# A two-layer attention and feed-forward kernel: other PSUM banks for the second projection, places of their own for its last copies, an earlier normalization, a maximum in two parts, and another order in the score rounds

## The chip, the cores and the metric

The kernel runs on one core of one Trainium2 chip. The metric is the device time of one execution in microseconds. Before the change it is 1984.87 us, the median of 3 runs that lie between 1984.5 and 1985.03 us.

## The reference

The input is one sequence of 2048 rows of 448 numbers. Attention has 16 query heads of width 28 that share one key and one value head of width 28. Two layers are run, each an attention block and then a gated feed-forward block, and both layers use the same weights:

```python
def _A_ref(x, wq, wk, wv, wo):
    q = (x @ wq).reshape(B, S, H, Dh).transpose(0, 2, 1, 3)
    k = x @ wk
    v = x @ wv
    scores = jnp.einsum("bhqd,bkd->bhqk", q, k) * (Dh ** -0.5)
    p = _softmax(scores, axis=-1)
    o = jnp.einsum("bhqk,bkd->bhqd", p, v)
    return o.transpose(0, 2, 1, 3).reshape(B, S, H * Dh) @ wo

def _B_ref(x, w_gate, w_up, w_down):
    return (_silu(x @ w_gate) * (x @ w_up)) @ w_down

x = A_x
for _ in range(2):
    x = x + _A_ref(_layernorm(x), A_wq, A_wk, A_wv, A_wo)
    x = x + _B_ref(_layernorm(x), B_w_gate, B_w_up, B_w_down)
```

`_layernorm` subtracts the mean of a row and divides by the root of its variance plus 1e-5. There is no scale and no bias.

## The kernel before

**Number formats.** A product in near-float32 precision is made of a high and a low part of each operand (`hi`, `lo`, type F32R) and three matmuls: high by high, high by low, low by high.

**Chunks.** The 2048 rows are four chunks (`c` = 0 to 3) of 512 rows, and a chunk is four tiles of 128 rows. PSUM has eight banks of 128 x 512 numbers. The order of the instructions on each engine is the order in which the program writes them (`manual_schedule`): there is no scheduler between, and an instruction that waits holds up all that stands behind it on its engine.

**The projection of a layer** (`project`, L493) has 16 steps, counted by `seen` from 0 to 15. Steps 4c to 4c+3 make one chunk's queries, keys and values: each is 11 matmuls of 128 x 512 into one bank (L312), which ScalarE then copies out twice, first the high part (L530), then the whole bank into a tile called `stage` (L531); SyncE's queue sends `stage` to DRAM (`qd`, and `kt` for the keys). Two of each chunk's four steps also have VectorE turn the value rows out of the bank (`vt`, L538), and GpSimd puts them into `vsb`. The order of the four steps in a chunk is `TURN` = (3, 2, 0, 1), and `LAST` = (1, 0, 2, 3) for chunk 3; the steps with a number below 2 are those that have a `vt`. `stage` has 3 buffers in layer 0 and 2 in layer 1.

The bank of a step comes from `bank(wide[-1], True)`, which takes the next free one of a list in turn; in the steps of `finish` the list is `ALL` = (4, 5, 6, 7, 0, 1, 2, 3). The last three steps take banks 3, 4 and 5:

```python
held, po = bank((3, 4, 5) if self.seen > len(self.order) - 4 else wide[-1], True)   # L516
```

**What stands between the steps.** `plan[n, 0]` is done ahead of step n and `plan[n, 1]` behind it. A chunk is normalized in parts (`norm_steps`, L211): `stat` for each of four tiles on VectorE (L217, L218), `scale` on GpSimd (L222 and, with a power of -0.5, L223), and `apply` for each of four tiles on VectorE (L230) with a small copy on GpSimd (L232). In layer 0 the statistics and the scale of chunk c stand behind step 4c-4 and the application behind step 4c-3. `flip` (L243) then turns the chunk by 16 transposes on TensorE (L248), ahead of the last step of the chunk before; ScalarE and VectorE split what they make into `xh` and `xl`. In layer 1 chunks 0 to 2 are turned on VectorE and sent through DRAM (`xt`); `parts` (L882, ahead of step 6 for chunk 2) splits what came back in `qstack`. Chunk 3 of layer 1 is applied ahead of step 8 (L857), and flipped ahead of step 11.

Steps 0 to 3 of layer 1 stand inside the last feed-forward groups of layer 0; steps 4 to 15 stand in `finish`, behind the last down-projection, whose sums lie in banks 4 to 7 until VectorE (L823) and ScalarE (L826) have taken them out.

`maxima` (L434) gives a bound on the scores of a chunk: 4 matmuls (L439), then on VectorE a transpose (L441), a reduction (L443), three small instructions (L447, L448, L450) and a DMA. For chunks 0 to 2 it stands behind steps 6, 10 and 14; for chunk 3 it stands between the first two cycles of the scores (L756).

**The scores** of a layer are 128 cycles, m = 0 to 127: 16 groups of queries by 8 cycles. A cycle (`cycle`, L613) handles two tiles of 128 keys. For each, `tile_scores` (L590) issues 3 rounds of 4 matmuls, one for each of four heads, in four row groups of the array (L597): heads 0 to 2 write the three banks of `three`, and head 3 writes a bank of its own, here called the single:

```python
for z, (kp, part) in enumerate(((0, 0), (1, 0), (0, 1))):
    for j in range(4):
```

ScalarE takes the exponential of each `three` (L619). VectorE copies each single into `pair` (L618), and ScalarE takes the exponential of both at once (L620). Behind the two tiles TensorE multiplies the probabilities of the cycle before by the values (`pv`, 16 matmuls, L652), and VectorE adds that up (L661, or a copy L659 in the first cycle of a group). There are two banks for all this, 6 and 7, and they change places in each cycle (`singles`, L609):

```python
return banks[6 + m % 2], banks[7 - m % 2]
```

The first tile's single and then, when VectorE has copied it, the product with the values go into the first of them; the second tile's single goes into the other, out of which VectorE first has to add up the product of the cycle before. Behind six of the cycles of the two layers TensorE also does an output projection (L582).

The feed-forward block after it is matmuls in two row groups (L332); the change does not touch it.

Of the kernel before, what the change touches and what calls it, by code (L numbers as in the profile page):

```python
# [8 lines left out]
F32 = mybir.dt.float32  # L9
# [6 lines left out]
P = 128  # L16
# [39 lines left out]
def forward(  # L56
# [81 lines left out]
    xres = pers.tile([P, NT, D], F32, name="xres")  # L138
    stats = pers.tile([P, NT, 6], F32, name="stats")
    mv = pers.tile([P, NT, 2], F32, name="mv")  # L140
    halfn = pers.tile([P, 4], F32, name="halfn")
    ident = pers.tile([P, P], F32, name="ident")
    vsb = pers.tile([P, NT, 32], F32, name="vsb")
    keys = [pers.tile([P, 2, 512], F32R, name=f"keys{c}") for c in range(NC)]
# [63 lines left out]
            again,  # L208
        )

    def norm_steps(c, pool=pers, twice=True):  # L211

        got = {}
        cs = slice(4 * c, 4 * c + 4)

        def stat(t):
            nc.vector.bn_stats(stats[:, 4 * c + t, :], xres[:, 4 * c + t, :])  # L217
            nc.vector.bn_aggr(mv[:, 4 * c + t, :], stats[:, 4 * c + t, :])  # L218

        def scale():  # L220
            rstd = pers.tile([P, 4], F32, name="rstd", bufs=2)
            nc.gpsimd.tensor_scalar(rstd, mv[:, cs, 1], 1.0, EPS, ALU.mult, ALU.add)  # L222
            nc.gpsimd.tensor_tensor(rstd, rstd, halfn, ALU.pow)  # L223
            got["r"] = rstd

        def apply(t):
            if t == 0:
                got["x"] = pool.tile([P, 4, 512], F32, name="xn")
            o, i, r = got["x"][:, t, 0:D], xres[:, 4 * c + t, :], got["r"][:, t : t + 1]
            nc.vector.tensor_scalar(o, i, mv[:, 4 * c + t, 0:1], r, ALU.subtract, ALU.mult)  # L230
            if twice:
                nc.gpsimd.tensor_copy(got["x"][:, t, D:512], o[:, 384:D])  # L232

        fs = [lambda t=t: stat(t) for t in range(4)] + [scale]
        return fs + [lambda t=t: apply(t) for t in range(4)], got

    def norm(c, pool=pers):
# [105 lines left out]
    class Attention:  # L343


        def __init__(self, layer):
            self.layer = layer
            self.squares = (0, 1, 2) if layer else ()
            self.X, self.norms, self.qd = {}, {}, {}
            self.done = 0  # L350
            self.order = [(c, m) for c in range(NC) for m in (TURN if c < NC - 1 else LAST)]
            self.seen = 0
            self.steps, self.places = [], []
            self.lent, self.plan = None, {}
            self.hi, self.rowsof, self.kt, self.when = {}, {}, {}, {}
            for c in range(NC):
                self.kt[c] = dram.tile([32, 512], F32, name=f"kt{layer}_{c}")
                self.at(4 * c + 4, lambda c=c: self.key_load(c))
                self.at(4 * c + 7, lambda c=c: self.key_split(c))
            for i in range(3):  # L360
                self.at(4 + 3 * i, lambda i=i: self.stack(i))
                self.at(6 + 3 * i, lambda i=i: self.parts(i))
# [70 lines left out]

        def maxima(self, c, pm=None):  # L434


            pm = bank(ALL)[1] if pm is None else pm
            for n, g in enumerate(TURN):
                nc.tensor.matmul(pm, kd[0:112, g, :], self.hi[c, g], start=(n == 0), stop=(n == 3))  # L439
            side = pers.tile([P, 512], F32, name="sg")  # L440
            nc.vector.transpose(side, pm)  # L441
            ng = pers.tile([P, 64], F32, name="ng")
            nc.vector.tensor_reduce(ng, side.rearrange("p (n k) -> p n k", k=8), AX.X, ALU.max, negate=True)  # L443
            two = pers.tile([P, 4, 2, 16], F32R, name="two")
            hi, lo = two[:, :, 0, :], two[:, :, 1, :]
            ng = ng.rearrange("p (b j) -> p j b", j=4)
            nc.vector.tensor_copy(hi, ng)  # L447
            nc.vector.tensor_tensor(lo, ng, hi, ALU.subtract)  # L448
            flat = pers.tile([P, P], F32, name="flat")
            nc.vector.transpose(flat, two.rearrange("p j z b -> p (j z b)").bitcast(F32))  # L450
            self.rowsof[c] = dram.tile([P, P], F32, name=f"rows{self.layer}_{c}")
            nc.sync.dma_start(self.rowsof[c], flat)

        def max_steps(self, i):

# [57 lines left out]
        def q(self, c, m):  # L513
            cs = slice(512 * c, 512 * c + 512)
            sq = c in self.squares
            held, po = bank((3, 4, 5) if self.seen > len(self.order) - 4 else wide[-1], True)  # L516
            ms = slice(P * m, P * m + P)
            wh, wl = self.w
            product_T(po, [wh[:, k, ms] for k in range(4)], [wl[:, k, ms] for k in range(4)], self.X[c])
            if not full and self.seen in (6, 10, 14):  # L520
                self.maxima(self.seen // 4 - 1)
            live.remove(held)
            if c not in self.qd:
                self.qd[c] = dram.tile([D, 512], F32, name=f"qd{self.layer}_{c}")
            raw = self.pool.tile([P, 512], F32, name="stage")
            if not full:
                if self.seen % 2 == 0:
                    self.two = wpool.tile([P, 2, 512], F32R, tag="wgh", name="q2", bufs=FG + 1)
                self.hi[c, m] = self.two[0:112, self.seen % 2, :]
                nc.scalar.copy(in_order(self.hi[c, m], sq), natural(po[0:112, :], sq))  # L530
            nc.scalar.copy(in_order(raw, sq), natural(po, sq))  # L531
# [6 lines left out]
            nc.vector.transpose(vt, po[96:128, :])  # L538
            vt = vt.rearrange("p (u t d) -> p u t d" if sq else "p (t u d) -> p u t d", t=4, u=4)
            for u in range(4):  # L540
                nc.gpsimd.tensor_copy(  # L541
                    vsb[32 * u : 32 * u + 32, 4 * c : 4 * c + 4, d0 : d0 + n], vt[:, u, :, 16 : 16 + n]
                )

        def finish(self):

            wide.append(ALL)
            if self.layer:
                nc.scalar.activation(warm, halfn[:, 0:1], AF.Exp)
            while self.seen < len(self.order):  # L550
                self.project()
            for n in sorted(self.when):
                for f in self.when[n]:
                    f()
            self.advance(len(self.steps), NM + KC * LEAD)
            wide.append(LOW)

        def scores(self, ff, xb):
            next(switch)
            inner = ExitStack()  # L560
            with tc.tile_pool(name=f"ow{self.layer}", bufs=1, side="right", reuse_waits="tile") as ow:
# [5 lines left out]
                todo, due = [], {}  # L567
# [22 lines left out]
                def tile_scores(n, three, one):  # L590
# [1 line left out]
                    i, kt = divmod(n, NT)  # L592
                    q, k, ks = qts[i % 3], keys[kt // 4], slice(P * (kt % 4), P * (kt % 4) + P)
                    for z, (kp, part) in enumerate(((0, 0), (1, 0), (0, 1))):
                        for j in range(4):
                            js = slice(32 * j, 32 * j + 32)
                            nc.tensor.matmul(  # L597
                                three[:, j, :] if j < 3 else one, k[js, kp, ks], q[js, part, :],
                                start=(z == 0), stop=(z == 2), tile_position=(32 * j, 0),
                            )  # L600
# [133 lines left out]
                for m in range(last):  # L734
# [11 lines left out]
                    if u == 4 and 10 < i <= 11 + FG:  # L746
                        ff.W[i - 11] = weights(i - 11)
                    cycle(m)
                    if m in due:
                        due.pop(m)()  # L750
                    if m in aside:
# [1 line left out]
                    if m:  # L753
                        pv(m - 1, singles(m)[0])
                    elif not full:
                        self.maxima(NC - 1, banks[6])  # L756
                    between_cycles(m)
                pv(last - 1, banks[6])
                self.lent = None
# [19 lines left out]
    class FeedForward:  # L779
# [61 lines left out]
        def hand_over(self, c):  # L841
# [7 lines left out]
            if c == NC - 1:  # L849
# [4 lines left out]
                    a.norms[c] = got  # L854

                a.X[c] = xtile(self.xbp)
                a.plan[8, 0] = [ready]  # L857
                return
            to = dram.tile([D, 512], F32, name=f"xt1_{c}")
            raw = [q.bitcast(F32)[:, z, :] for q in qts[:2] for z in range(2)]  # L860
# [181 lines left out]
    if mask is not None:  # L1042
        nc.gpsimd.memset(mask, 0.0)
        nc.gpsimd.memset(mask[:, 0:16:5, :], 1.0)
        for base, sign in ((0, 1), (DH - 1, -1)):
# [2 lines left out]
                base=base, channel_multiplier=sign,  # L1048
            )
    parts[1]()  # L1050
    for c in range(1, NC):
        fs, got = norm_steps(c)
        n = 4 * c - 4
        at.plan[n, 1] = fs[:5]
        at.plan[n + 1, 1] = fs[5:] + [lambda c=c, got=got: at.norms.__setitem__(c, got)]
    for layer in range(2):
        at.finish()
        xb.close()
# [33 lines left out]
```

## Time and profile before

| | |
|---|---|
| median of 3 runs | 1984.87 us (1984.5 to 1985.03) |
| the profiled execution, as timed | 1986.38 us |
| its span, first to last instruction | 1984.7 us |
| mean granted TensorE clock | 0.996 |
| TensorE matmul busy | 1960.1 us, 99% |
| ScalarE busy | 1270.1 us, 64% |
| VectorE busy | 968.9 us, 49% |
| GpSimd busy | 555.3 us, 28% |
| projection of layer 0, scores of layer 0 | from 0 and from 63.84 us |
| steps 4 to 15 of the projection of layer 1, scores of layer 1 | from 1004.72 and from 1044.60 us |

All times in rows are microseconds from the start of the span unless they are marked ns. PE is TensorE (PEld its weight loads), ACT is ScalarE, DVE is VectorE, POOL is GpSimd, and SP is SyncE, which here issues DMAs. A row of the timeline gives the start, the duration, the engine, the line, the operation, what it writes and reads, the shape and how many instructions in a row were merged; in brackets stands how long the engine was idle before it and what ended that. Matmuls overlap, so that the distance from one start to the next is the cost, not the duration. In a row of the stretches stand the length and then the busy time of each engine, and as third number from the end the granted TensorE clock as a share of full speed.

### The profile page before, as it was taken

To read this page: it belongs to the slowest core of one execution; us is meant where nothing else is said; L and a number is where in the kernel's file an instruction comes from. 1 tells how busy PE (TensorE), PEld (TensorE's weight loads), DVE (VectorE), ACT (ScalarE), POOL (GpSimd) and SP (SyncE) were. 2 spreads that over 40 slices of the span, in tenths; PEclk is the share of its full clock that TensorE was granted. 3 is DMA by queue.
4 is the path that set the end of the run, shared out by engine and by line. 5 is a ranking of instruction groups with operands and counts; after the bars stand their busy time and mean duration, and the time that the engine had idled before them with its cause. 6 is when DMAs were issued, how large, how long until landed. Compare 5 with 4: busy or idle time off the path is not lost. (4 is left out here: it accounts for less than half of the span.)

```text
span 1984.7 us, 43786 instructions
## 1 busy us (share of the span) xinstructions
PE 1960.1 (99%) x18469; PEld 1337.4 (67%) x18469; DVE 968.9 (49%) x1638; ACT 1270.1 (64%) x1888; POOL 555.3 (28%) x597
## 2 busy tenths in 40 slices
PE   9999999999999999999999999999999999999998
PEld 7544545445468999999974445454454789988886
DVE  6656565665743223222665565656657432222222
ACT  4899797997953333333348997979979433333332
POOL 5222113122214333333331221122221242333320
PEclk9999999999999999999999999999999999999999
DMA  5101011021030011110241010200211301011102
GB/s 165 54 23 33 18 36 39 19 54 31 24 84 26 17 32 32 32 32 22 79 134 35 26 31 12 62 12 23 51 48 26 74 17 32 17 31 32 32 1 76
DMA packets 99875, 80.50 MB, mean 41 GB/s; under 512 B 25848, under 2 KB 82296, under 8 KB 99672
## 3 DMA queue, kind: packets, MB, share of 16 engines
q1 hardware_dynamic: 98120, 76.44, 14.2%
q8 instruction: 146, 2.39, 0.5%
q10 hardware_dynamic: 1552, 1.20, 0.2%
q14 instruction: 57, 0.47, 0.1%
HBM read 56.24 MB, written 20.58 MB: 39 GB/s over the span
## 5 line engine op out<-in xcount | busy, mean ns | idle before, releaser
L619 ACT ACTIVATE pt<-three 128x1536 f32<-128x1536 f32 x512 | 714.9, 1449 | 65.7 <-PE three L597 62.4
L652 PE MATMUL bank<-pt,vsb 128*32 128x512 f32 x3072 | 490.8, 598 | 1.9 <-DVE pair L618 1.2
L652 PE MATMUL bank<-pair,vsb 128*32 128x512 f32 x1024 | 487.4, 598 | 0.5 <-ACT pair L620 0.5
L597 PE MATMUL bank<-qstack,keys 32*128 32x512 f32 x1536 | 471.9, 426 | 1.7 <-DVE xres L586 1.7
L332 PE MATMUL bank<-xh,wgh 64*128 64x512 f32 x1728 | 448.7, 389 | 0.0
L597 PE MATMUL three<-qstack,keys 32*128 32x512 f32 x4608 | 430.4, 409 | 2.5 <-ACT stage L531 2.5
L597 PEld LDWEIGHTS three<-qstack,keys 32*128 32x128 f32 x4608 | 262.8, 183 | 232.2 <-issue 203.0
L618 DVE COPY pair<-bank 128x512 f32<-128x512 f32 x512 | 353.8, 691 | 100.7 <-PE bank L597 71.6
L332 PE MATMUL bank<-xh,wgl 64*128 64x512 f32 x1404 | 370.3, 390 | 0.0
L332 PE MATMUL bank<-xl,wgh 64*128 64x512 f32 x1296 | 336.5, 389 | 0.0
L332 PE MATMUL bank<-wdh,h 64*128 64x448 f32 x1792 | 333.6, 363 | 1.7 <-ACT h L945 0.8
L944 DVE TENSOR_TENSOR sg<-bank,sg 128x512 f32<-128x512 f32 x112 | 77.4, 691 | 502.8 <-ACT sg L943 498.6
L332 PEld LDWEIGHTS bank<-xh,wgh 64*128 64x128 f32 x1728 | 265.7, 184 | 16.6 <-issue 1.3
L652 PEld LDWEIGHTS bank<-pt,vsb 128*32 128x32 f32 x3072 | 101.7, 109 | 253.2 <-issue 153.2
L620 ACT ACTIVATE pair<-pair 128x1024 f32<-128x1024 f32 x256 | 271.8, 1062 | 0.0
L597 PEld LDWEIGHTS bank<-qstack,keys 32*128 32x128 f32 x1536 | 245.1, 184 | 37.0 <-DVE o L659 5.2
L827 POOL TENSOR_TENSOR xres<-stage,xres 128x448 f32<-128x448 f32 x108 | 127.3, 1197 | 502.8 <-ACT stage L826 502.5
L332 PEld LDWEIGHTS bank<-wdh,h 64*128 64x128 f32 x1792 | 247.3, 184 | 15.2 <-issue 2.0
L661 DVE TENSOR_TENSOR o<-bank,o 128x512 f32<-128x512 f32 x224 | 154.7, 691 | 209.1 <-PE bank L652 209.1
L339 ACT COPY seen<-bank 128x1 f32<-128x1 f32 x664 | 82.1, 163 | 250.6 <-PE bank L332 247.6
L332 PEld LDWEIGHTS bank<-xh,wgl 64*128 64x128 f32 x1404 | 218.7, 184 | 14.1
L332 PE MATMUL bank<-wdl,h 64*128 64x448 f32 x896 | 221.1, 367 | 0.0
(133 smaller groups left out, 2120.9 us busy)
## 6 DMA issues: line engine op xcount, KB each, us to landing
o<-rd SPq DMA_DIRECT2D x32, 256.0 KB
qd<-stage SPq DMA_DIRECT2D x32, 224.0 KB
qraw<-qd SPq DMA_DIRECT2D x128, 56.0 KB
wdr<-in_B_w_down_dram SPq DMA_DIRECT2D x28, 224.0 KB
xt<-tb SPq DMA_DIRECT2D x24, 224.0 KB
wr<-in_B_w_gate_dram SPq DMA_DIRECT2D x28, 192.0 KB
wr<-in_B_w_up_dram SPq DMA_DIRECT2D x28, 192.0 KB
xn<-xt SPq DMA_DIRECT2D x6, 768.0 KB
```

The costliest lines, as they stand in the source:

```text
L332: nc.tensor.matmul(po, a, b, start=start, stop=stop, skip_group_check=True)
L339: nc.scalar.copy(seen[:, i : i + 1], po[:, 0:1])
L597: nc.tensor.matmul(three[:, j, :] if j < 3 else one, k[js, kp, ks], q[js, part, :], start=(z == 0), stop=(z == 2), tile_position=(32 * j, 0),)
L618: copies.append(nc.vector.tensor_copy(pt1, one))
L619: es.append(nc.scalar.activation(pt, threes[y], AF.Exp, scale=SCALE))
L620: es.append(nc.scalar.activation(pair, pair, AF.Exp, scale=SCALE))
L652: nc.tensor.matmul(to[32 * j : 32 * j + 32, :], vsb[:, n % NT, :], pts[n][j], start=(y == 0), stop=(y == 1), skip_group_check=True,)
L661: f = nc.vector.tensor_tensor(accs[i][:, 0, :], to, accs[i][:, 0, :], ALU.add)
L827: nc.gpsimd.tensor_tensor(r, s, r, ALU.add)
L944: nc.vector.tensor_tensor(in_order(sg, sq), natural(pg[1], sq), in_order(sg, sq), ALU.mult)
```

## The change

It has six parts, and the rest is as before.

1. In `tile_scores` the rounds of every tile with an even number (the first of each cycle) issue head 3, the single, ahead of heads 0 to 2. The second tile's order stays.
2. `maxima` is cut in two: the matmuls and the first transpose at once, and the reduction, the small instructions and the DMA in a function that it returns. For chunks 0 to 2 that is called at once; for chunk 3 it is called behind the two tiles of cycle 1.
3. In layer 0 the statistics of chunks 2 and 3 are all taken behind step 4, with one `scale` of 128 x 8 numbers for both (`halfn` is widened for it). Those of chunk 3 stood behind step 8. The application of each chunk stays where it was.
4. In layer 1 chunk 3 is applied behind step 5 rather than ahead of step 8.
5. In layer 1 the list of banks in `finish` is (0, 1, 2, 3, 4, 5, 6, 7). With it step 4 takes bank 0 (it was 4), and step 11 takes bank 3 and step 12 bank 4 (they were 1 and 2). The last three steps still take 3, 4 and 5.
6. In layer 1 the four copies L531 of chunk 3 go to four places of the tile `xn` rather than to the two buffers of `stage`.

```diff
-    halfn = pers.tile([P, 4], F32, name="halfn")
+    halfn = pers.tile([P, 8], F32, name="halfn")
...
-    def norm_steps(c, pool=pers, twice=True):
+    def norm_steps(c, pool=pers, twice=True, chunks=1):
...
-        cs = slice(4 * c, 4 * c + 4)
+        cs = slice(4 * c, 4 * c + 4 * chunks)
...
-            rstd = pers.tile([P, 4], F32, name="rstd", bufs=2)
+            rstd = pers.tile([P, 4 * chunks], F32, name=f"rstd{chunks}", bufs=2)
             nc.gpsimd.tensor_scalar(rstd, mv[:, cs, 1], 1.0, EPS, ALU.mult, ALU.add)
-            nc.gpsimd.tensor_tensor(rstd, rstd, halfn, ALU.pow)
+            nc.gpsimd.tensor_tensor(rstd, rstd, halfn[:, 0 : 4 * chunks], ALU.pow)
...
-        fs = [lambda t=t: stat(t) for t in range(4)] + [scale]
+        fs = [lambda t=t: stat(t) for t in range(4 * chunks)] + [scale]
...
             side = pers.tile([P, 512], F32, name="sg")
             nc.vector.transpose(side, pm)
-            ng = pers.tile([P, 64], F32, name="ng")
-            nc.vector.tensor_reduce(ng, side.rearrange("p (n k) -> p n k", k=8), AX.X, ALU.max, negate=True)
...
+            def least_rows():
+                ng = pers.tile([P, 64], F32, name="ng")
+                nc.vector.tensor_reduce(ng, side.rearrange("p (n k) -> p n k", k=8), AX.X, ALU.max, negate=True)
...
+                nc.sync.dma_start(self.rowsof[c], flat)
+
+            return least_rows
...
             if not full and self.seen in (6, 10, 14):
-                self.maxima(self.seen // 4 - 1)
+                self.maxima(self.seen // 4 - 1)()
...
-            raw = self.pool.tile([P, 512], F32, name="stage")
+            if self.layer and c == NC - 1:
+                if "xn" not in self.spare:
+                    self.spare["xn"] = pers.tile([P, 4, 512], F32, name="xn")
+                raw = self.spare["xn"][:, self.seen % 4, :]
+            else:
+                raw = self.pool.tile([P, 512], F32, name="stage")
...
-            wide.append(ALL)
+            wide.append((0, 1, 2, 3, 4, 5, 6, 7) if self.layer else ALL)
...
-                        for j in range(4):
+                        for j in (0, 1, 2, 3) if n % 2 else (3, 0, 1, 2):
...
                     cycle(m)
+                    while m and late:
+                        late.pop()()
...
                     elif not full:
-                        self.maxima(NC - 1, banks[6])
+                        late.append(self.maxima(NC - 1, banks[6]))
...
-                a.plan[8, 0] = [ready]
+                a.plan[5, 1] = [ready]
...
+    two = {}
     for c in range(1, NC):
-        fs, got = norm_steps(c)
+        fs, got = norm_steps(c, chunks=2 if c == 2 else 1)
         n = 4 * c - 4
-        at.plan[n, 1] = fs[:5]
-        at.plan[n + 1, 1] = fs[5:] + [lambda c=c, got=got: at.norms.__setitem__(c, got)]
+        if c == 2:
+            two = got
+            at.plan[n, 1] = fs[:9]
+        elif c == 1:
+            at.plan[n, 1] = fs[:5]
+        else:
+            at.plan[n, 1] = [lambda got=got: got.__setitem__("r", two["r"][:, 4:8])]
+        at.plan[n + 1, 1] = fs[-4:] + [lambda c=c, got=got: at.norms.__setitem__(c, got)]
```

More of the change, by code (lines that the diff above doesn't have):

```diff
@@ L349, in __init__ @@
             self.X, self.norms, self.qd = {}, {}, {}
-            self.done = 0
+            self.done, self.spare = 0, {}
             self.order = [(c, m) for c in range(NC) for m in (TURN if c < NC - 1 else LAST)]
@@ L441, in maxima @@
             nc.vector.transpose(side, pm)
-            ng = pers.tile([P, 64], F32, name="ng")
[L443 to L452, printed above, removed]
+            def least_rows():
+                ng = pers.tile([P, 64], F32, name="ng")
+                nc.vector.tensor_reduce(ng, side.rearrange("p (n k) -> p n k", k=8), AX.X, ALU.max, negate=True)
+                two = pers.tile([P, 4, 2, 16], F32R, name="two")
+                hi, lo = two[:, :, 0, :], two[:, :, 1, :]
+                ng = ng.rearrange("p (b j) -> p j b", j=4)
+                nc.vector.tensor_copy(hi, ng)
+                nc.vector.tensor_tensor(lo, ng, hi, ALU.subtract)
+                flat = pers.tile([P, P], F32, name="flat")
+                nc.vector.transpose(flat, two.rearrange("p j z b -> p (j z b)").bitcast(F32))
+                self.rowsof[c] = dram.tile([P, P], F32, name=f"rows{self.layer}_{c}")
+                nc.sync.dma_start(self.rowsof[c], flat)
+            return least_rows
         def max_steps(self, i):
@@ L566, in scores @@
                 on, accs, pts = {}, {}, {}
-                todo, due = [], {}
+                todo, due, late = [], {}, []
                 def load_wo(z):
```

## The prediction

> **What bounds the kernel now.** First the page's head, then the table of stretches for a piece of the scores of layer 1 (length, then busy time of PE, PEld, DVE, ACT, POOL, the granted clock, DMA share, GB/s).
>
> ```profile
> span 1984.7 us, 43786 instructions
> PE 1960.1 (99%) x18469; PEld 1337.4 (67%) x18469; DVE 968.9 (49%) x1638; ACT 1270.1 (64%) x1888; POOL 555.3 (28%) x597
> ```
>
> ```profile
> 1300.00:1400.00 100.00, 99.63 (x1031) 48.67 (x1023) 61.25 (x107) 89.52 (x74) 20.35 (x21) 1.00 0.07 17
> ```
>
> TensorE looks like the bound, but 99% hides waits, since the modelled ends overlap. So I read the timeline of one cycle, start to start:
>
> ```profile
> 1351.64 0.50 PE L597 MATMUL three<-qstack,keys 32*128 32x512 f32 x3
> 1351.77 0.69 DVE L661 TENSOR_TENSOR o<-bank,o 128x512 f32<-128x512 f32 x1 [0.47 <-PE bank L652]
> 1352.20 0.39 PE L597 MATMUL three<-qstack,keys 32*128 32x512 f32 x3
> 1352.22 0.39 PE L597 MATMUL bank<-qstack,keys 32*128 32x512 f32 x1
> 1352.65 1.45 ACT L619 ACTIVATE pt<-three 128x1536 f32<-128x1536 f32 x1
> 1352.68 0.69 DVE L618 COPY pair<-bank 128x512 f32<-128x512 f32 x1 [0.22 <-PE bank L597]
> 1353.08 0.39 PE L597 MATMUL bank<-qstack,keys 32*128 32x512 f32 x1
> 1353.43 0.12 PEld L652 LDWEIGHTS bank<-pt,vsb 128*32 128x32 f32 x3 [0.39 <-DVE pair L618]
> 1353.43 0.63 PE L652 MATMUL bank<-pt,vsb 128*32 128x512 f32 x3
> 1355.29 0.51 PE L597 MATMUL three<-qstack,keys 32*128 32x512 f32 x3
> ```
>
> The period is 1355.29 - 1351.64 = 3.65 us. Inside it runs a loop of two engines. The last round of the first tile's single starts at 1352.22 and frees the copy L618 at 1352.68. That ends at 1353.37, and the product, which goes into the same bank, starts at 1353.43 and names the copy as what it waited for. From product to next scores, 1.86 us, TensorE issues without a wait. ScalarE is busy for 90% of the stretch, and its exponential L619 starts 0.03 us ahead of the copy, as heads 0 to 2 are issued 0.02 us ahead of the single.
>
> **Part 1, the single first.** Nothing is added; in 256 cycles the copy is freed sooner. How much: ahead of the single's last matmul there is now one semaphore event, that of `three`, and it costs the copy the 0.03 us between 1352.65 and 1352.68. The Trainium skill, page "TensorE: Matmul & The Clock Gate", section "The cost: per-tile semaphore tail", says that back-to-back matmuls serialize their semaphore increments at 26.3 ns each. That agrees with the 0.03 us here; by issue order alone it would be the 0.02 us between 1352.20 and 1352.22.
>
> The copy's 0.03 us can't all be kept, for TensorE must also finish the second tile's last single, which starts at 1353.08, 0.35 us ahead of the product. How short that can get shows a cycle whose sum came late:
>
> ```profile
> 1341.70 0.69 DVE L618 COPY pair<-bank 128x512 f32<-128x512 f32 x1 [0.15 <-PE bank L597]
> 1342.17 0.39 PE L597 MATMUL bank<-qstack,keys 32*128 32x512 f32 x1
> 1342.49 0.63 PE L652 MATMUL bank<-pt,vsb 128*32 128x512 f32 x3
> ```
>
> The copy was over at 1342.39, and the product still came 0.32 us behind the single. In ordinary cycles that distance is 0.34 to 0.35 us, here in the first and in the last of the 207 that the trace has:
>
> ```profile
> 77.14 0.39 PE L597 MATMUL bank<-qstack,keys 32*128 32x512 f32 x1
> 77.48 0.63 PE L652 MATMUL bank<-pt,vsb 128*32 128x512 f32 x3
> 1542.94 0.39 PE L597 MATMUL bank<-qstack,keys 32*128 32x512 f32 x1
> 1543.28 0.63 PE L652 MATMUL bank<-pt,vsb 128*32 128x512 f32 x3
> ```
>
> So 0.34 - 0.32 = about 0.02 us is to be had, 207 times: **-4.3 us** with 0.021 (bounds 0 and, with the whole 0.025, -5). The 29 late cycles (1342.49 above) are bound by the sum and gain nothing; the rest are starts of layers and cycles with an output projection, counted at nothing for the same reason.
>
> **Part 2, maxima in two parts.** Cycle 1 of layer 0:
>
> ```profile
> 67.58 1.08 ACT L620 ACTIVATE pair<-pair 128x1024 f32<-128x1024 f32 x1
> 67.96 0.69 DVE L443 TENSOR_REDUCE ng<-sg 128x64 f32<-128x512 f32 x1
> 68.53 2.81 ACT L619 ACTIVATE pt<-three 128x1536 f32<-128x1536 f32 x2
> 69.23 0.31 DVE L450 STREAM_TRANSPOSE flat<-two 128x128 f32<-128x128 f32 x1
> 69.47 1.25 DVE L618 COPY pair<-bank 128x512 f32<-128x512 f32 x2
> 70.18 0.63 PE L652 MATMUL bank<-pt,vsb 128*32 128x512 f32 x3 [1.23 <-DVE pair L618]
> ```
>
> Four instructions, from 67.96 to 69.47, lie ahead of the two copies, and the product waited 1.23 us. With them behind the copies the first copy waits for its single alone, some 1.3 us sooner, and the product comes at about 68.9. The four, about 1.5 us, then stand ahead of the copy L659 that empties the product's bank, and who waits for that is the second single of the next cycle: I reckon 0.4 us given back. **-0.9 us** (-0.4 to -1.3) per layer; layer 1's is inside the sum of parts 4 to 6. Their DMA goes 1.3 us later on SP's queue; the rows that it brings are used only in chunk 3's groups, 12 x 8 cycles of 3.65 us, 350 us, later, so that costs nothing.
>
> **Part 3, statistics of chunk 3 with chunk 2.** This goes the wrong way.
>
> ```profile
> 29.09 0.62 DVE L217 BATCH_NORM_STATS2 stats<-xres 128x6 f32<-128x448 f32 x1
> 31.92 0.18 DVE L218 BATCH_NORM_AGGREGATE mv<-stats 128x2 f32<-128x6 f32 x1
> 32.54 1.01 POOL L223 TENSOR_TENSOR rstd<-rstd,halfn 128x4 f32<-128x4 f32 x1
> 33.59 1.78 DVE L230 TENSOR_SCALAR xn<-xres,mv,rstd 128x448 f32<-128x448 f32 x4 [1.49 <-POOL rstd L223]
> 35.02 2.05 PE L248 MATMUL bank<-ident,xn 128*128 128x128 f32 x16
> ```
>
> Statistics of four tiles take VectorE from 29.09 to 32.10, of which 2.9 us are work (4 x 0.73). Four more now stand ahead of the application L230, which is 1.5 us behind the end of the statistics for the power on GpSimd. The power on twice the columns is between 0 and 0.8 us longer (if the 1.01 us were all proportional it would be 1.0, less a fixed part); I take 0.4. The flip's first matmul is at 35.02, on the heels of L230: there is no slack, and TensorE stalls for 2.9 + 0.4 = 3.3 us. TensorE then has no wait longer than a part of a us up to the scores, so that the whole is carried to the end. Chunk 3's later flip gains some 0.2 us. A stall of this length is also followed by a slower clock, shown under parts 4 to 6, 1.0 us (0 to 1.7, half of one such row of 3.42 us). Sum **+4.1 us** (2.7 to 5.5).
>
> **Parts 4 to 6, projection of layer 1.**
>
> ```profile
> 1016.16 0.50 PE L312 MATMUL bank<-xh,wh 128*128 128x512 f32 x1 [0.21 <-ACT xh L292]
> 1028.73 0.85 PE L248 MATMUL bank<-ident,xn 128*128 128x128 f32 x4 [1.90 <-POOL xn L232]
> 1033.25 0.69 DVE L264 TENSOR_TENSOR xh<-bank,xh 64x512 fp32r<-64x512 f32 x1
> 1036.07 0.39 PE L312 MATMUL bank<-xh,wh 128*128 128x512 f32 x1
> 1036.63 0.72 DVE L538 STREAM_TRANSPOSE vt<-bank 32x512 f32<-32x512 f32 x1 [2.69 <-ACT stage L531]
> 1044.60 0.50 PE L597 MATMUL three<-qstack,keys 32*128 32x512 f32 x3
> 1047.80 0.80 PE L597 MATMUL three<-qstack,keys 32*128 32x512 f32 x3 [2.23 <-ACT stage L531]
> ```
>
> The other bank lets step 4 start some 2 us sooner, ahead of VectorE's L823. But step 8 (1016.16) waits for ScalarE's split of chunk 2, which nothing here moves: what is gained ahead of it is waited for there. The earlier application of chunk 3 takes away the 1.90 us at 1028.73, on POOL's queue past steps 6 and 7; but step 12 needs the flipped chunk split, and that ended at 1033.25 + 0.69 = 1033.94 behind ScalarE's copies, which stay. So this gain stops at step 12 too. Then a new wait: step 13 (1036.07) takes bank 3, which step 11 now used, and step 11's bank is not free until L538 is over, 1036.63 + 0.72 = 1037.35. Step 13 starts 1.3 us later, and behind it stand steps 14, 15 and the scores. The places of their own remove the 2.23 us at 1047.80, and with it a price beyond its length:
>
> ```profile
> 1044.03:1047.45 3.42, 1.54 (x15) 0.69 (x13) 1.16 (x3) 0.88 (x2) 1.33 (x5) 1.00 0.51 169
> 1047.45:1054.27 6.82, 6.47 (x40) 3.84 (x40) 3.33 (x7) 5.23 (x5) 1.25 (x1) 0.50 0.22 74
> ```
>
> The clock was 0.50 for the 6.82 us after it, in which TensorE was busy 6.47. That can have cost up to half of 6.47, 3.2 us; I take 1.7, as TensorE also waits for ScalarE (5.23 us busy) there. With the new stall of about 2.9 us ahead of step 13 I expect a slow stretch there instead, of one row's length (3.42 us at half speed, 1.6 lost). Scores that start 1.3 + 1.6 = 2.9 us later than 1044.60, -2.2 for the wait, -1.7 for the slow stretch behind it, -0.9 for part 2: **-1.9 us** (-3.5 with the full clock at step 13; -0.5 if the old slow stretch cost 0.3).
>
> **Sum.** -4.3 - 0.9 + 4.1 - 1.9 = -3.0. The profiled span of 1984.7 would become 1981.7; the median of the runs is 1984.87, 0.17 above the span, so 1984.87 - 3.0 = **1981.9 us**. A change under 0.2%, 4 us, can hardly be told from none.
>
> **Rivals.**
>
> *The clock stays up.* The Trainium skill, page "TensorE: Matmul & The Clock Gate", section "HAM oscillation — how this bites in real kernels", asks for no TensorE idle gap above about 3.4 us. By that rule stalls of 2.9 to 3.3 us would not slow the clock. The trace speaks against it, as the wait of 2.23 us was followed by 0.50. Worked out from the rows: if the new stalls are not followed by a slow clock and the power is no longer for 8 columns, part 3 costs 2.9 - 0.2 = 2.7, layer 1 gives -3.5, the rest stands: -6.0, **1978.9 us**, faster.
>
> *The loop gains nothing.* If something else holds the product (the end of the single's last matmul itself, with the 0.34 us as its floor and the late cycles 0.32 by chance), part 1 is 0: -3.0 + 4.3 = +1.3, **1986.2 us**, no change.
>
> *ScalarE is the bound of the cycle, slower.* L620 to L619 is 0.97 us (1351.68 to 1352.65), and L619 starts as soon as `three` is told complete. With the single first, that comes second and 0.03 us later. If ScalarE's three instructions are what sets the 3.65 us, each of 236 cycles (207 + 29) is 0.03 longer: +7.1 rather than -4.3, in all +8.4, **1993.3 us**. It decides if ScalarE has under 0.03 us of slack. Against it: L620 to L619 took 0.95 (67.58 to 68.53) where the scores were long done, so that ScalarE can do 0.02 us better than it does; and TensorE names the copy, not ScalarE. For it: ScalarE's 90%.
>
> **How the numbers follow.** Forecast 0.42 (about a quarter of it beyond -0.2%), clock stays up 0.25, loop gains nothing 0.18, ScalarE 0.07, and 0.08 for sizes off in either direction. Faster: 0.10 + 0.22 + 0.04 = 0.36. Slower: 0.07 + 0.03 + 0.04 = 0.14. The same: 0.50. The range runs from 1977.5 (the clock case with the loop at -5 and part 2 at -1.3 is 1977.8) to 1988.5 (part 1 at nothing, part 3 at its upper bound of 5.5, layer 1 at -1.0: +3.6).
>
> **What would show it.** Right: the distance from second single to product 0.32 us, the copy ahead of L619, the period 3.63; in cycle 1 of layer 0 the product some 0.4 us behind L619's start rather than 1.65; L230 of chunk 2 at 36.9 and the scores of layer 0 at about 68; step 13 of layer 1 naming L538, and no wait of the second tile on L531. Wrong: a period above 3.65, or a wait of TensorE on L620 or L619 that was not there; the flip ahead of step 7 still on time; a slow clock in some other stretch of layer 1.

## The result, and the profile after

| | before | after |
|---|---|---|
| median of 6 runs | 1984.95 us | 1973.39 us |
| ratio | | 0.9941, 95% interval 0.9928 to 0.9954 |
| span of the profiled execution | 1984.7 us | 1971.3 us |

The change makes the kernel 11.6 us faster, four times the forecast 3.0 us and outside the range. The page of the changed kernel:

```profile
span 1971.3 us, 43781 instructions
PE 1943.9 (99%) x18469; PEld 1340.4 (68%) x18469; DVE 967.6 (49%) x1638; ACT 1260.6 (64%) x1888; POOL 554.1 (28%) x595
```

It says no more than the page of before: the same matmuls, 99% busy. Where the time came from shows only a table by stage, made from the starts of the same instructions in both traces (us):

| stage | before | after | difference | forecast |
|---|---|---|---|---|
| start to cycle 3 of layer 0 (projection, maxima) | 75.69 | 79.70 | +4.0 | +3.2 |
| cycle 3 to the last product, layer 0 | 491.73 | 489.59 | -2.1 | -2.1 |
| feed-forward of layer 0, to step 0 of layer 1 | 413.50 | 409.33 | -4.2 | 0 |
| step 0 to cycle 3, layer 1 | 79.04 | 74.81 | -4.2 | -1.9 |
| cycle 3 to the last product, layer 1 | 491.88 | 489.59 | -2.3 | -2.2 |
| feed-forward of layer 1, to the end | 432.81 | 428.29 | -4.5 | 0 |

The two feed-forward blocks, whose code the change does not touch, gave 8.7 us. The stretches show it best: 300 us inside the last block, first of before, then of after. After the length come PE's busy time and, in brackets, its number of matmuls.

```profile
1600.00:1900.00 300.00, 300.00 (x2704) 269.73 (x2703) 87.94 (x127) 99.24 (x372) 99.82 (x82) 1.00 0.10 26
```

```profile
1600.00:1900.00 300.00, 300.00 (x2744) 273.06 (x2742) 87.75 (x126) 97.57 (x376) 101.49 (x84) 1.00 0.09 26
```

TensorE is busy all the time and at full clock in both, waits for nothing, and yet does 2744 matmuls where it did 2704: 1.5% more. The groups by line say the same of one kind of matmul (mean ns is the second number behind the bar), before and after:

```profile
L332 PE MATMUL bank<-xh,wgl 64*128 64x512 f32 x1404 | 370.3, 390 | 0.0
```

```profile
L332 PE MATMUL bank<-xh,wgl 64*128 64x512 f32 x1404 | 340.8, 386 | 0.0
```

Each of these matmuls is 4 ns shorter, but their ends are modelled, so the starts say more. From start to start in one row group the matmuls by the gate and up weights (`wgh`, `wgl`) were 231, 231 and 228 ns apart in before (medians over 1294 to 1708 steps of each of the three kinds of product) and 227 in after; the mean over all 4507 steps is 230.3 and 227.0 ns. The matmuls of the down-projection (`wdh`, `wdl`) hardly changed, 204.9 and 204.2. The matmuls of the projections, which use all rows and run one at a time, are 227 ns apart in both.

The loop of the scores, timeline of after:

```profile
1341.97 0.63 PE L660 MATMUL bank<-pt,vsb 128*32 128x512 f32 x3
1344.38 0.39 PE L605 MATMUL bank<-qstack,keys 32*128 32x512 f32 x1
1344.82 0.69 DVE L626 COPY pair<-bank 128x512 f32<-128x512 f32 x1 [0.16 <-PE three L605]
1344.88 2.79 ACT L627 ACTIVATE pt<-three 128x1536 f32<-128x1536 f32 x2
1345.28 0.39 PE L605 MATMUL bank<-qstack,keys 32*128 32x512 f32 x1
1345.60 0.63 PE L660 MATMUL bank<-pt,vsb 128*32 128x512 f32 x3
```

(Lines below the change are some 8 higher than in before: L626 is the copy that was L618, L627 the exponential, L660 the product. The releaser named behind the copy is inferred; the copy reads the single alone.) The copy now starts 0.06 us ahead of the exponential, the product 0.32 us behind the second single, and from product to product it is 3.63 us. Over the trace: 3.627 us in 214 ordinary cycles, before 3.649 in 207.

Cycle 1 of layer 0 after:

```profile
73.26 0.69 DVE L626 COPY pair<-bank 128x512 f32<-128x512 f32 x1 [0.17 <-PE three L605]
73.69 2.81 ACT L627 ACTIVATE pt<-three 128x1536 f32<-128x1536 f32 x2
74.03 0.63 PE L660 MATMUL bank<-pt,vsb 128*32 128x512 f32 x3
74.75 0.67 DVE L444 TENSOR_REDUCE ng<-sg 128x64 f32<-128x512 f32 x1
76.25 0.65 DVE L667 COPY o<-bank 128x512 f32<-128x512 f32 x1
76.96 0.18 PEld L605 LDWEIGHTS bank<-qstack,keys 32*128 32x128 f32 x1 [0.22 <-DVE o L667]
```

The product stands 0.34 us behind L627 (it was 1.65); the four instructions from 74.75 on delay L667, for which the second single waits 0.22 us.

The front of layer 0, and layer 1's projection:

```profile
35.40 1.64 POOL L223 TENSOR_TENSOR rstd<-rstd,halfn 128x8 f32<-128x8 f32 x1
37.08 1.78 DVE L230 TENSOR_SCALAR xn<-xres,mv,rstd 128x448 f32<-128x448 f32 x4 [2.13 <-POOL rstd L223]
37.65 4.30 PE L248 MATMUL bank<-ident,xn 128*128 128x128 f32 x16 [2.52 <-DVE xn L230]
```

```profile
1012.38 0.59 ACT L539 COPY stage<-bank 128x512 f32<-128x512 f32 x1 [5.07 <-DMA qd<-stage]
1012.87 1.66 ACT L292 CAST xh<-qstack 128x512 fp32r<-128x512 f32 x3
1013.52 1.89 DVE L293 TENSOR_TENSOR xl<-qstack,xh 128x512 fp32r<-128x512 f32 x3 [3.86 <-ACT xh L292]
1016.17 0.72 DVE L440 STREAM_TRANSPOSE sg<-bank 128x512 f32<-128x512 f32 x1
1017.03 0.76 PE L312 MATMUL bank<-xh,wh 128*128 128x512 f32 x1 [5.75 <-DVE sg L440]
1026.98 1.91 PE L248 MATMUL bank<-ident,xn 128*128 128x128 f32 x16
1034.07 0.50 PE L312 MATMUL bank<-xh,wh 128*128 128x512 f32 x1
1043.96 0.51 PE L605 MATMUL three<-qstack,keys 32*128 32x512 f32 x3 [0.26 <-ACT xn L539]
```

The first is as forecast in kind: L230 at 37.08, the power 0.6 us longer where 0.4 was taken, the flip late and slow. In the second a wait stands that I had not seen: step 8 waits 5.75 us, and what ends last is not chunk 2 but the maxima's transpose L440. ScalarE's part of the splitting of chunk 2 (L292), behind a copy that waited 5.07 us for a transfer out of `stage`, was over at 1014.53, 2.5 us ahead of step 8.

### The profile page after: what moved, and what is told of

Same layout as the page of the kernel before. It is cut to its first block, busy times and chain, and to the rows that moved or that the text cites. A ratio compares the mean times of both kernels' runs of the same rounds, so it can differ in the third digit from the quotient of the medians.

```text
span 1971.3 us, 43781 instructions
## 1 busy us (share of the span) xinstructions
PE 1943.9 (99%) x18469; PEld 1340.4 (68%) x18469; DVE 967.6 (49%) x1638; ACT 1260.6 (64%) x1888; POOL 554.1 (28%) x595
## 4 chain that ended last, share of the span: by engine, by line
PE 95%; DVE 1%; DMA 1%; POOL 1%; ACT 1%; issue 1%; SPq 0%; ACTq 0%; POOLq 0%; DVEq 0%
PE bank L332 40%; PE bank L660 24%; PE bank L605 17%; PE three L605 5%; PE bank L312 3%; PE three L590 2%; PE bank L590 2%; PE bank L248 1%; DMA kt<-stage 0%; PE bank L438 0%; DVE stats L217 0%; DMA xd<-xh 0%; POOL vsb L549 0%; DMA xres<-in_A_x_dram 0%; DVE pair L626 0%
## 5 line engine op out<-in xcount | busy, mean ns | idle before, releaser
L627 ACT ACTIVATE pt<-three 128x1536 f32<-128x1536 f32 x512 | 727.2, 1500 | 63.5 <-PE three L605 42.3
L660 PE MATMUL bank<-pt,vsb 128*32 128x512 f32 x3072 | 490.8, 598 | 0.4
L660 PE MATMUL bank<-pair,vsb 128*32 128x512 f32 x1024 | 487.4, 598 | 0.6 <-ACT pair L628 0.6
L332 PE MATMUL bank<-xh,wgh 64*128 64x512 f32 x1728 | 405.5, 387 | 0.0
L626 DVE COPY pair<-bank 128x512 f32<-128x512 f32 x512 | 354.3, 692 | 99.3 <-PE bank L605 62.4
L332 PE MATMUL bank<-xh,wgl 64*128 64x512 f32 x1404 | 340.8, 386 | 0.0
L332 PE MATMUL bank<-wdh,h 64*128 64x448 f32 x1792 | 322.4, 362 | 1.4 <-ACT h L955 0.8
L332 PE MATMUL bank<-xl,wgh 64*128 64x512 f32 x1296 | 303.3, 386 | 0.0
L628 ACT ACTIVATE pair<-pair 128x1024 f32<-128x1024 f32 x256 | 285.5, 1115 | 0.0
L660 PEld LDWEIGHTS bank<-pt,vsb 128*32 128x32 f32 x3072 | 101.7, 109 | 246.7 <-issue 153.2
L669 DVE TENSOR_TENSOR o<-bank,o 128x512 f32<-128x512 f32 x224 | 155.0, 692 | 204.2 <-PE bank L660 204.2
L332 PEld LDWEIGHTS bank<-xh,wgh 64*128 64x128 f32 x1728 | 225.7, 184 | 13.7 <-issue 1.3
L332 PEld LDWEIGHTS bank<-wdh,h 64*128 64x128 f32 x1792 | 217.7, 183 | 13.0 <-issue 2.0
L953 ACT ACTIVATE sg<-bank 128x512 f32<-128x512 f32 x112 | 67.1, 599 | 213.2 <-PE bank L332 210.5
L332 PE MATMUL bank<-wdl,h 64*128 64x448 f32 x896 | 199.1, 364 | 0.0
```

Of the source, the lines that this page charges most:

```text
L332: nc.tensor.matmul(po, a, b, start=start, stop=stop, skip_group_check=True)
L626: copies.append(nc.vector.tensor_copy(pt1, one))
L627: es.append(nc.scalar.activation(pt, threes[y], AF.Exp, scale=SCALE))
L628: es.append(nc.scalar.activation(pair, pair, AF.Exp, scale=SCALE))
L660: nc.tensor.matmul(to[32 * j : 32 * j + 32, :], vsb[:, n % NT, :], pts[n][j], start=(y == 0), stop=(y == 1), skip_group_check=True,)
L669: f = nc.vector.tensor_tensor(accs[i][:, 0, :], to, accs[i][:, 0, :], ALU.add)
```

## The experiments

### Why the feed-forward blocks are faster

The wider `rstd` of part 3 is a new tile, 2 buffers of 32 bytes per partition. All tiles that are allocated behind it (weights, `xh`, `xl`, `xd`, `pt`, `pair`, `stage`) lie 64 bytes higher in the built program. My theory "places" was that this sets the pace; the rival "entry" that the pace depends on how TensorE enters the block.

**e1**, before with nothing but the shift:

```diff
             rstd = pers.tile([P, 4], F32, name="rstd", bufs=2)
+            if c == 2:
+                pers.tile([P, 16], F32, name="gap")
```

> The kernel before, with nothing but an unused tile of 64 bytes per partition allocated ahead of the tiles that the change's wider rstd tile pushed up by 64 bytes (weights, xh, xl, pt, pair and others). Theory 'places': the feed-forward matmuls run at 227 rather than 230 ns a pair because of these addresses, so this kernel alone gains the 8.7 us that the two feed-forward blocks gained: 1976.2 us, with 2744 matmuls in a 300 us stretch of the last feed-forward block rather than 2704. Rival 'entry': the pace is set by how TensorE enters the block (phase of the two row groups, stalls ahead of it), which this kernel leaves as before: 1985 us and 2704.

Measured: 1975.51 us, ratio 0.9953 (0.9939 to 0.9967).

```profile
1600.00:1900.00 300.00, 300.00 (x2741) 272.66 (x2739) 88.84 (x128) 98.31 (x372) 99.67 (x82) 1.00 0.09 27
```

An unused tile of 64 bytes brings 9.4 us. "Entry" has fallen: TensorE enters as before (3.648 us a cycle), and the pace is the new one.

**e2**, after with another 64 bytes (`if chunks == 2:` and the same tile):

> The changed kernel with another unused 64 bytes, so that the same tiles lie 128 bytes higher than before. 'Places', if what counts is the address modulo 128: feed-forward back at the pace of before, 1973.4 + 8.7 = 1982.1 us. 'Places', if any start but the old one is quick: 1973.4. 'Entry': 1973.4.

Measured: 1972.38 us, 0.9941 (0.9927 to 0.9955). Quick as well, so it is not the address modulo 128.

**f1**, e1 with 64 words (256 bytes) rather than 16:

> The kernel before with an unused tile of 256 bytes per partition in the place of the 64 bytes that gained 9 us. If the start modulo 256 (or 128, or 64) bytes sets the pace, the feed-forward blocks go back to 2704 matmuls in the 300 us stretch and the kernel to 1985 us. If the old places are slow for their distance to tiles that do not move (h2, keys, vsb lie below them), any shift is quick: 2744 and 1976 us.

Measured: 1984.68 us, 1.0002 (0.9992 to 1.0011).

```profile
1600.00:1900.00 300.00, 300.00 (x2708) 270.69 (x2708) 87.77 (x126) 98.32 (x367) 98.52 (x80) 1.00 0.10 26
```

At 256 bytes the old pace is back: the start modulo 256 counts.

**f2**, before with the gap behind the weights, so that only the moving operands shift, and **f6**, the reverse: the weights by 64, the moving operands by 64 + 192 = 256:

```diff
         dl = wpool.tile([P, D], F32R, name="wdl", bufs=FG + 1)
+        if fc == 0:
+            wpool.tile([P, 16], F32, name="gap")     # f2; in f6 [P, 48], with e1's gap ahead of the weights
```

> The kernel before with the 64 bytes allocated behind the feed-forward weights, so that only the moving operands xh, xl, xd (and pt, pair, stage) lie higher and the weights wgh, wgl, wdh, wdl stay. If the moving operand's start sets the pace: quick, 1976 us, 2744 matmuls. If the weights' start sets it: 1985 us, 2704. If both matter in part: between, 1980.

> The kernel before with 64 unused bytes ahead of the feed-forward weights and 192 behind them, so that the weights lie 64 bytes higher (128 modulo 256) and the moving operands xh, xl, xd 256 bytes higher (64 modulo 256, as before). If the weights' start alone sets the pace: quick, 2741 matmuls in the 300 us stretch and 1976 us. If both operands must be off the slow start: 2706 and 1985 us.

Measured: 1985.46 us, 1.0003 (0.9994 to 1.0012), and 1988.03 us, 1.0014 (1.0005 to 1.0023). First f2, then f6:

```profile
1600.00:1900.00 300.00, 300.00 (x2706) 271.30 (x2707) 88.38 (x127) 99.35 (x373) 99.61 (x82) 1.00 0.09 26
```

```profile
1600.00:1900.00 300.00, 300.00 (x2696) 259.49 (x2695) 87.78 (x127) 98.76 (x372) 100.34 (x82) 1.00 0.10 26
```

Neither alone does it: whichever operand stays at 64 while the other is at 128, the pace stays slow.

**f3, f5, f7, f8**, e1 with 8, 48, 24 and 40 words: the remaining starts but one.

> The kernel before with 32 unused bytes, so that xh, xl and the weights start 96 bytes past a multiple of 128 rather than 64. If only starts of 64 modulo 256 are slow: 1976 us. If every start off a multiple of 128 is slow (64 slow, 0 quick; the 64 that was quick lay at 192 modulo 256, against this): 1985 us.

> The kernel before with 192 unused bytes: xh, xl and the weights start at 0 modulo 256. So far, with both operands moved alike: 64 and 96 slow, 128 and 192 quick. If starts in the upper half of 256 bytes are the quick ones: slow, 2705 matmuls in the 300 us stretch and 1985 us. If 64 is an exception among the multiples of 64: quick, 2741 and 1976 us.

> The kernel before with 96 unused bytes: xh, xl and the weights start at 160 modulo 256. If starts in the upper half of 256 bytes are quick: 2741 and 1976 us. If a start has to be a multiple of 64 (the 96 that was slowest was none): 2696 and 1987 us.

> The kernel before with 160 unused bytes: xh, xl and the weights start at 224 modulo 256. If starts in the upper half of 256 bytes are quick: 2741 and 1976 us. If a start has to be a multiple of 64: 2696 and 1987 us.

All together, with the starts from the built program (moving operands / weights):

| kernel | starts modulo 256 | matmuls in 300 us | median us |
|---|---|---|---|
| f5 | 0 / 0 | 2690 | 1989.14 |
| before | 64 / 64 | 2704 | 1984.95 |
| f1 | 64 / 64 (256 higher) | 2708 | 1984.68 |
| f3 | 96 / 96 | 2696 | 1987.64 |
| f2 | 128 / 64 | 2706 | 1985.46 |
| f6 | 64 / 128 | 2696 | 1988.03 |
| e1 | 128 / 128 | 2741 | 1975.51 |
| f7 | 160 / 160 | 2751 | 1975.54 |
| e2 (of after) | 192 / 192 | 2748 | 1972.38 |
| f8 | 224 / 224 | 2737 | 1979.25 |

The two ends, f5 and f7:

```profile
1600.00:1900.00 300.00, 300.00 (x2690) 261.32 (x2691) 87.44 (x126) 98.83 (x371) 99.29 (x82) 1.00 0.09 26
```

```profile
1600.00:1900.00 300.00, 300.00 (x2751) 274.18 (x2749) 89.44 (x129) 97.92 (x372) 99.27 (x81) 1.00 0.10 27
```

"Multiples of 64" has fallen (0 is slowest, 160 quickest). Starts in the upper half of 256 bytes are quick, those in the lower half slow, and 224 is a little slower; 32 was not tried. The mean step of the gate and up matmuls was 226.7 to 227.5 ns with starts of 128, 160 and 192, 228.7 with 224, and 230.3 to 232.3 in the six slow kernels; that of the down-projection, whose operand `h` stays at 224 in all of them, was 202 to 206 ns without so clear a step. Why the chip does this is not shown, nor whether it holds where the two operands' starts differ in other ways than in f2 and f6.

### What the parts are worth

**e3**, after without part 3, with `gap` in the place of the wider tile so that no address changes:

```diff
-        fs, got = norm_steps(c, chunks=2 if c == 2 else 1)
+        fs, got = norm_steps(c)
...
+        at.plan[n, 1] = fs[:5]
+        at.plan[n + 1, 1] = fs[5:] + [lambda c=c, got=got: at.norms.__setitem__(c, got)]
```

> The changed kernel without part 3 (statistics of chunks 2 and 3 each in their old place), with an unused tile of 64 bytes where the wider rstd tile lay, so that all addresses stay. My step for part 3: the flip of chunk 2 on time again, scores of layer 0 from about 63.8 us rather than 69.0, so 1973.4 - 5.2 = 1968.2 us. Rival: the early time is given back in the scores or the feed-forward block, 1973.4.

Measured: 1968.82 us, 0.9922 (0.9908 to 0.9935), scores of layer 0 from 63.84 us. Part 3's own work costs 4.6 us, with the clock behind its stall as it fell in the runs of after. **g1**, the same with `gap` of 128 bytes:

> The changed kernel without part 3, with 128 unused bytes: the version that the runs so far point to. The 128 bytes were about 1.0 us quicker than the 64 in the changed kernel, so 1968.8 - 1.0 = 1967.8 us. If that 1.0 us was the front stall's luck (scores of layer 0 from 66.8 rather than 69.0 in that run): 1968.8 us.

Measured: 1969.97 us, 0.9925 (0.9911 to 0.9939): no gain over e3.

**e4**, after with `for j in range(4)` in the score rounds again:

> The changed kernel with the four matmuls of each score round in their old order. My step for part 1: period of a cycle 3.649 rather than 3.627 us in some 210 cycles, 1973.4 + 4.5 = 1977.9 us. Rival, that the shorter period comes from the changed addresses of pt and pair or from elsewhere: 1973.4.

Measured: 1977.71 us, 0.9964 (0.9951 to 0.9978), 3.649 us in the ordinary cycles. Part 1 is worth 4.3 us.

**h1, h2, h3**, each e3 with one more part undone:

```diff
-            wide.append((0, 1, 2, 3, 4, 5, 6, 7) if self.layer else ALL)
+            wide.append(ALL)                       # h1, part 5
-            if self.layer and c == NC - 1:
+            if False:                              # h2, part 6
-                a.plan[5, 1] = [ready]
+                a.plan[8, 0] = [ready]             # h3, part 4
```

> The changed kernel without part 3 (addresses kept, 1968.8 us) and without part 5: the old list of banks in the second projection. By my step, what step 4 gains ahead of L833 is waited for at step 8: no change, 1968.8 us. Rival, the gain of 2.4 us reaches the scores of layer 1: 1971.2 us.

Measured: 1965.43 us, 0.9899 (0.9884 to 0.9915), 3.4 us *faster* than e3. Neither "no change" nor a gain for part 5 has come out: part 5 is a loss. The timeline of h1 at steps 4 and 8 (its lines are 2 higher than in after):

```profile
997.66 0.51 PE L314 MATMUL bank<-xh,wh 128*128 128x512 f32 x1 [2.30 <-DVE xres L835]
...
1009.55 0.50 PE L314 MATMUL bank<-xl,wh 128*128 128x512 f32 x1 [0.23 <-DVE xl L295]
```

Step 4 waits 2.30 us again, but step 8 waits for hardly anything. The built program shows why. The maxima behind step 6 take their bank from `ALL`, which counts by itself once the steps have a list of their own, and get bank 4; step 8 is then given bank 4 too, and must wait until L440 has read it, which stands on VectorE behind its part of the splitting of chunk 2 (L293). The wait has a price behind it as well: the granted clock of after was 0.50 from 1016.52 to 1019.94. With one list for both, the maxima have bank 7 and step 8 has bank 1.

> The changed kernel without part 3 and without part 6: the last copies of chunk 3 go to the two buffers of stage again. By my step the second tile of the scores of layer 1 waits some 2.2 us again and a slow clock follows, 1.7 us: 1968.8 + 3.9 = 1972.7 us. Rival, with the other parts the transfers out of stage are early enough: 1968.8 us.

Measured: 1971.00 us, 0.9926 (0.9913 to 0.9940), so part 6 is worth 2.2 us by the runs:

```profile
1040.72 0.50 PE L607 MATMUL three<-qstack,keys 32*128 32x512 f32 x3 [0.74 <-ACT stage L541]
1043.08 1.45 ACT L629 ACTIVATE pt<-three 128x1536 f32<-128x1536 f32 x1 [1.06 <-DMA kt<-stage]
1044.59 0.50 PE L607 MATMUL three<-qstack,keys 32*128 32x512 f32 x3 [0.87 <-ACT pt L629]
```

The wait comes back with 0.74 us in place of 2.23, and a second one behind it, since ScalarE's next exponential stands behind a transfer out of `stage`; no stretch there ran at half clock.

> The changed kernel without part 3 and without part 4: chunk 3 of layer 1 is normalized ahead of step 8 again. By my step the flip's wait of 1.9 us comes back and would be hidden at step 12: 1968.8 us. By the profile of the changed kernel, in which step 12 waits for nothing, it and the slow clock behind it are paid, 1.9 + 1.7: 1972.4 us.

Measured: 1968.45 us, 0.9918 (0.9903 to 0.9933). No difference: with step 8 late anyway, the flip is in time either way. What part 4 is worth with the old banks, where step 8 is not late, was not run.

**j1**, h1 with part 2 undone (`self.maxima(NC - 1, banks[6])()` between the cycles):

> The changed kernel without parts 3 and 5 (1965.4 us) and without part 2: the maxima of chunk 3 whole again, between the cycles. By my step and by cycle 3's start in the profiles, 0.9 to 1.2 us a layer come back: 1965.4 + 2.2 = 1967.6 us. Rival, that the second cycle's wait moves to the sum behind it and costs the same: 1965.4 us.

Measured: 1968.34 us, 0.9911 (0.9895 to 0.9928): part 2 is worth 2.9 us for both layers by the runs, 1.1 us in each layer by the traces (below).

h1, the change without parts 3 and 5 but with their 64 bytes, is the fastest version: 1965.43 us, 1% less than before.

## Why the prediction was wrong

By the runs, each against its neighbour: addresses -9.4, part 1 -4.3, part 2 -2.9, part 3 +4.6, part 4 0, part 5 +3.4, part 6 -2.2. That is -10.8 of the measured -11.6 us. The intervals of the ratios are some 3 us wide to each side, and the kernel before, run beside them, had medians from 1984.16 to 1985.36 us, so the small ones lean on the traces:

| piece | compared | part |
|---|---|---|
| first score to cycle 3, both layers | j1 11.82 and 11.82 us, h1 10.71 and 10.70 | part 2: -2.2 |
| first score to cycle 3, layer 1 | h2 12.22, e3 10.71 | part 6: -1.5 |
| step 0 to the first score, layer 1 | e3 63.95, h1 61.27 | part 5: +2.7 |
| step 0 to the first score, layer 1 | e3 63.95, h3 64.16 | part 4: -0.2 |

In h2 and j1 the piece from step 0 to the first score is 1.2 and 1.0 us longer than in e3 and h1, and it is so ahead of what parts 6 and 2 touch. There the clock differed: 0.58, 0.50 and 0.92 in three stretches of 3.42 us from 1010.52 in h2 where e3 had 0.50, 0.79 and 1.00, and, behind the same wait of 2.3 us ahead of step 4, 0.50 in j1 where h1 had 1.00.

**The step that failed** is one that the prediction did not make: it held the feed-forward blocks to be untouched. Part 3 was costed as work on VectorE and GpSimd, and its new tile as nothing. That tile's 64 bytes, which move the operands of the feed-forward matmuls, were worth twice the work, with the other sign: e1, which has them and nothing else, gained 9.4 us. Without them the sum would have been near, -11.6 + 9.4 = -2.2 against -3.0, but in part by luck, since errors inside parts 3 to 6 cancel.

**Part 1, right.** -4.3 forecast, -4.3 measured, with the floor of 0.32 us between second single and product that the late cycles had shown. By this the rivals "the loop gains nothing" and "ScalarE is the bound" have fallen. The copy is ahead of the exponential by 0.06 us rather than behind it by 0.03. The Trainium skill (page "TensorE: Matmul & The Clock Gate", section "The cost: per-tile semaphore tail") gives 26.3 ns for an increment. In the trace the three matmuls of heads 0 to 2 make one increment together and the single makes one, so that one stands between the two in either order: 0.03 us is about one, as the page has it, and 0.06 is about two, which it does not explain.

**Part 2, right:** -0.9 us a layer forecast, -1.1 in each layer's trace; the -2.9 of the runs can't be told from that. Cycles 1 and 2 of layer 0 take 79.70 - 72.27 = 7.43 us rather than 75.69 - 67.10 = 8.59.

**Part 3, right in sum:** +4.1 forecast, +4.6 measured. L230 came 3.5 us later (37.08 rather than 33.59), but TensorE waited 2.52 us, not 3.3: there was some slack after all. The slow clock took about 2.2 us, going by e2 below (69.00 - 66.83), where 1.0 was allowed. The clock in it is luck, as the stretches of after, then of e2, show behind the same stall:

```profile
37.62:41.04 3.42, 3.40 (x13) 2.67 (x14) 3.25 (x8) 1.17 (x2) 1.43 (x4) 0.50 0.01 2
```

```profile
37.62:41.04 3.42, 2.88 (x18) 2.27 (x19) 3.29 (x8) 1.53 (x4) 1.44 (x4) 1.00 0.01 2
```

After 2.5 us without a matmul the clock was 0.50 in after and 0.58 in e4, and 1.00 in e2, whose scores of layer 0 began at 66.83 rather than 69.00. The rule of the Trainium skill (page "TensorE: Matmul & The Clock Gate", section "HAM oscillation — how this bites in real kernels") asks for no TensorE idle gap above about 3.4 us. Gaps of 2.5 us keep to it, and the clock stayed up in one of three. The rival built on it, 1978.9 us, would have been nearer, but not for its reason.

**Parts 4 to 6, right sign by chance.** That step 8 takes back what step 4 gains was right, but by another wait, and it takes back more: the wait is for L440, not for chunk 2's split. The wait of step 13 for L538 was all but absent: step 13 starts at 1034.07, 0.3 us late. Probably the pause at step 8 let the transfers out of `stage` drain, so that ScalarE was no longer late with step 11; no run tests that. The flip at 1026.98 waits for nothing, and step 12 neither. The loss forecast for part 5 (2.9 us at step 13) has the size of the one that came at step 8, so the sum of this layer looks better than its mechanism was.

What part 6 removes was 1.5 to 2.2 us, not 3.9, at least behind the pause at step 8. The 3.9 was read from one execution, and this place is not fixed: in the nine kernels here whose second projection is that of before (before, e1 and the seven f runs) layer 1 takes 1.3 to 4.2 us more than layer 0 from the first score to cycle 3, and 3.5 in the profile of before. From step 0 to cycle 3 of layer 1 the nine take 76.1 to 79.0 us, and the profiled execution of before had the longest; the 74.81 of after is 1.3 to 4.2 us less. The parts as undone one by one come to about nothing there, so they do not simply add up: parts 4 and 6 were measured behind the pause that part 5 makes.

## What to carry to other kernels

In this kernel a new tile moved every tile allocated behind it: after an edit, compare the pace of the code that was *not* edited, in matmuls for a full stretch, before explaining the difference by the code that was. To judge an edit by itself, hold the addresses with an unused tile of the same size. Where two places draw from one set of buffers, they have to draw from one counter, or one will be given what the other still reads.

## What the runs showed of the hardware that I had not expected

Two matmuls side by side in row groups of 64 rows ran at 227 ns a step on average when both operands started at 128, 160 or 192 in 256 bytes, at 228.7 when both started at 224, and at 230 to 232 ns when both started at 0, 64 or 96, or one at 64 and the other at 128, at full clock and without a wait in the profile: up to 2.3% of the matmuls in a stretch (2690 to 2751). Matmuls on all 128 rows kept 227 ns in before and after. The power on 8 columns took 1.64 us, on 4 columns 1.01. A stall of 2.5 us at one and the same place was followed by a clock of 0.50 and 0.58 in two runs and by full clock in a third, and one of 2.3 us at another place by 0.50 in one run and 1.00 in another.
